# An attention and gated-convolution kernel: weights decoded two chunks per instruction, and the smaller part of x made in PSUM for two units

## Chip, cores and metric

The kernel runs on one core of a Trainium2 chip. What counts is the device time of one execution in microseconds (us), from outside; beside it stands the span, from the first to the last instruction of a profiled execution.

## Reference

Attention over a sliding window of 64 positions, then a feed-forward block with a three-tap convolution as gate. All data are float32; the weights arrive as 64-bit floats (two 32-bit words each) and are decoded on the chip.

```python
def _attn_ref(q, k, v):                      # batch 8, heads 8, seq 576, head_dim 64
    scores = scale * np.matmul(q, k.transpose(0, 1, 3, 2))
    mask = (rel >= 0) & (rel < 64)
    scores = np.where(mask, scores, -1000000000.0)
    scores = scores - np.max(scores, axis=-1, keepdims=True)
    attn = np.exp(scores)
    attn = attn / (np.sum(attn, axis=-1, keepdims=True) + 1e-09)
    return np.matmul(attn, v)
def _moe_ref(x, w_in, conv_w, w_out):        # x: (8, 576, 512), d_ff 1024
    h = np.maximum(x @ w_in, 0.0)
...
    for k in range(K):
        conv_out += conv_w[k][None, None, :] * hp[:, k:k + S, :]
    gate = 1.0 / (1.0 + np.exp(-conv_out))
    return (h * gate @ w_out)
```

## The kernel before

**Units and stages.** The 4608 rows of x are worked in 12 units of 384 rows. Of each unit, `scores` (L538) multiplies queries by keys, `row_max` (L559, VectorE) adds the mask and takes the maximum, `exps` (L569, ScalarE) makes exponentials and their sums, `guard`, `reciprocal` and `normalise` (L575 to L588) divide, and the result is turned so that keys lie on the partitions: for units 0 and 1 by TensorE (`turn`, L595) and a copy out of PSUM (`unturn`, L600), for the later ones by VectorE (`transpose`, L607) and 12 small DMAs (`place`, L620). `values` (L627) then makes x, one of four chunks c of 128 features per PSUM bank.

**Split operands.** TensorE works on float32r here, a float32 of fewer bits, so every operand is split into a larger and a smaller part. `split_hi` (L632) copies the bank of x to `xh` on ScalarE or VectorE, and `split_lo` (L637) subtracts `xh` from the bank on VectorE and writes `xl`. `mm1` (L644) is 12 matmuls for one of eight chunks f of d_ff: larger times larger, larger weight-rest times larger x, and larger weight times `xl`. Then come `relu` (L670, L672), the convolution (`conv_mid`, `conv_side`, L686 to L693), `sigmoid` (L697), `gate` (L704), the split of the gated values (`gate_hi` L709, `gate_lo` L714) and `mm2` (L723, L728), three matmuls per piece. `result` (L733) copies the banks out, and SyncE stores them.

**Decoding a weight chunk.** A chunk f of w_in or w_out is 128 by 512 numbers, each two words. `load_w` (L426) fetches it; then `magnitude` (L438 ScalarE or L440 VectorE), `shift` (L444, VectorE), `sign` (L448, VectorE), `low` (L451, ScalarE), `add_low` (L455, VectorE), `larger` (L471, any of three engines) and `lo` (L475, VectorE or GpSimd). In `DECODE` the first two chunks of w_in stand alone, all others in pairs; of a pair only `shift` is one instruction, the rest are one per chunk. The decoded chunk takes the memory of its raw words.

**Order.** `plan()` lists every piece of work, and the string `ORDER` gives the order in which they are written out, by number; a letter after a number picks the engine (A ScalarE, D VectorE, P GpSimd), `/n` the PSUM bank, and `F5/0` stands for 5 matmuls on spare data (`fill`, L404). Each engine works its own part of this list strictly in order, and SyncE's part is the order of the loads. Tasks go: unit 0 with chunks 0 to 3, unit 1 with chunks 0 to 3, unit 0 with 4 to 7, unit 1 with 4 to 7, then units 2 to 11 whole. So decoding, the attention of units 0 to 3 and the first matmuls all lie in the first 90 us.

Of the kernel before, what the change touches and what calls it, by code (L numbers as in the profile page):

```python
# [15 lines left out]
P = 128  # L16
# [6 lines left out]
NT = 6  # L23
# [14 lines left out]


# [83 lines left out]
def plan():  # L123
# [126 lines left out]
    224P 240 93P 151A 77/1 231 225 70 152P 75D 232 76 213 78D 226P 468 79 146A 316 73 199 242 215P 233P 206 82  # L250
    F5/2 94/0 147D 241 207P 249 119A 234 120D 123 243P 216 83 121 208/4 250 105/1 122 251 235D 252A 209A 217D
    469 84 128 127 153/7 168 317A 244 200 85 253 245P 96D 318A 106D 107A 254D 3 321 227/5 108 110A 218/6 319
    236/4 155A 111 219A 255/0 326 109 473/2 228A 112 470 246/1 256A 325 367 113 260/7 346 124 169 129 257/0 396
    125P 474 237A 258D 114P 247A 259 261A 475 F3/6 263/1 158A 477 262 266/0 270 320 484/2 327 126D 156/7 264A
    633 322 267A 345 115A 328D 323P 265 170A 268 116P 130A 485 269/1 174 486 157A 161A 131D 179 159 509/2 479
    329D 133/5 171A 324D 634 271A 162 272/0 366 476 172 472 487 173 178 478 290/7 175 273A 480D 163 490 274D 488
    275 136 481 635 160 277A 397 293/1 482P 510 489 471 511 176A 491A 512 278 134/6 177P 492 483 164 132/4 180
    495 137 279 639/2 372 636 165D 369A 135 520 276 166A 330/0 493D 181A 280 167D 513 182P 640 183 508 185 291
    494 281P 186 292D 368A 501 188 641 351 500 184 514 370 507 187 294A 376 502 282A 650/2 371 505 295A 283P
# [100 lines left out]
def attention_moe(ctx: ExitStack, tc: tile.TileContext, q, k, v, first, w_in, conv_w, w_out, out):  # L360
# [96 lines left out]
    def part(buf, j):  # L457
        return wx[buf][:, j * DM:(j + 1) * DM]
# [391 lines left out]
```

## Time and profile before

| | us |
|---|---|
| median of 3 runs | 514.12 (513.76 to 515.83) |
| the profiled execution | 513.32 |
| its span | 511.5 |
| TensorE (PE) busy | 499.8 |
| VectorE (DVE) busy | 398.7 |
| ScalarE (ACT) busy | 327.1 |
| GpSimd (POOL) busy | 169.2 |

The profiled execution took 513.32 us, 1.8 us more than its span and 0.8 us less than the median of the runs. In the rows below PE is the matmuls and PEld the loads of their stationary operand; times are in us from the start of the span, and L is a line of the kernel. What stands in brackets behind a row is the engine's idle time just before it and what ended it. The duration of an instruction on DVE and ACT overlaps the start of the next, so the price of one in a full queue is the distance between two starts.

### The profile page before, as it was taken

The numbers are of one execution on the slowest core, as the hardware profiler recorded it, in microseconds if no ns is written. First come the engines' busy times: TensorE is split into PE (matmuls) and PEld (weight loads), VectorE is DVE, ScalarE is ACT, GpSimd is POOL, SyncE is SP. The second block draws the span as 40 slices with busy tenths as digits, with TensorE's granted clock in tenths as the row PEclk, the third lists the DMA queues.
The fourth block names the chain that finished last, engine by engine and source line by source line (L and its number), as shares of the span: only waits on it lengthen the run. The fifth ranks groups of instructions, "written<-read, shape, count | busy, mean of one in ns | idle before, by whom it ended". The sixth has DMA issues, their size and how long they took to land.

```text
span 511.5 us, 13953 instructions
## 1 busy us (share of the span) xinstructions
PE 499.8 (98%) x5375; PEld 438.2 (86%) x5375; DVE 398.7 (78%) x1197; ACT 327.1 (64%) x923; POOL 169.2 (33%) x254
## 2 busy tenths in 40 slices
PE   8798999999999999999999999999999999999997
PEld 5587978998888898898888889988889889898996
DVE  5999999997996986597667858887386778846682
ACT  5999999967837863855864874572792675242330
POOL 6766452430441442511332532121344131152020
PEclk9999999999999999999999999999999999999999
DMA  8996635082634533804642613806263303410011
GB/s 326 405 408 216 257 84 146 6 288 85 161 104 114 175 70 105 261 4 125 212 144 70 219 62 112 258 14 197 59 254 110 108 13 113 124 62 33 0 63 62
DMA packets 27570, 71.98 MB, mean 141 GB/s; under 512 B 5744, under 2 KB 14064, under 8 KB 27504
## 3 DMA queue, kind: packets, MB, share of 16 engines
q1 hardware_dynamic: 27216, 69.52, 40.8%
q0 software_dynamic: 288, 1.57, 1.8%
q8 instruction: 42, 0.69, 0.6%
q14 instruction: 24, 0.20, 0.1%
HBM read 48.26 MB, written 11.01 MB: 116 GB/s over the span
## 4 chain that ended last, share of the span: by engine, by line
PE 87%; DVE 9%; POOL 2%; issue 1%; ACT 0%; POOLq 0%
PE bank L723 36%; PE bank L644 36%; PE bank L627 7%; PE bank L538 5%; PE bank L728 3%; DVE s L559 2%; DVE c L693 1%; DVE wx L448 1%; DVE xl L637 1%; POOL s L588 1%; DVE wx L455 1%; DVE s L588 1%; DVE wx L444 0%; ACT s L569 0%; POOL mask L493 0%
## 5 line engine op out<-in xcount | busy, mean ns | idle before, releaser
L644 PE MATMUL bank<-xh,w_in 128*128 128x384 f32 x768 | 197.5, 338 | 0.0
L723 PE MATMUL bank<-w_out,gh 128*128 128x512 f32 x528 | 168.8, 401 | 0.0
L644 PEld LDWEIGHTS bank<-xh,w_in 128*128 128x128 f32 x768 | 138.8, 188 | 7.0
L693 DVE SCALAR_TENSOR_TENSOR c<-hbuf,cw,c 128x386 f32<-128x386 f32 (+1 forms) x192 | 125.0, 674 | 13.8 <-ACT c L686 12.5
L644 PE MATMUL bank<-xl,w_in 128*128 128x384 f32 x384 | 129.0, 336 | 0.9 <-DVE xl L637 0.9
L569 ACT ACTIVATE s<-s,nm 128x96 f32<-128x96 f32 (+2 forms) x288 | 105.2, 368 | 17.1 <-DVE nm L559 16.9
L723 PEld LDWEIGHTS bank<-w_out,gh 128*128 128x128 f32 x528 | 96.0, 188 | 19.0 <-POOL w_out L475 0.2
L723 PE MATMUL bank<-w_out,gl 128*128 128x512 f32 x264 | 104.2, 395 | 0.2 <-DVE gl L714 0.2
L704 POOL TENSOR_TENSOR c<-c,hbuf 128x386 f32<-128x386 f32 (+5 forms) x39 | 44.8, 1166 | 110.4 <-ACT c L697 110.4
L559 DVE CUSTOM_DVE_ANT_0 s<-bank,mask 128x96 f32<-128x96 f32 (+2 forms) x288 | 56.6, 255 | 29.3 <-PE bank L538 25.1
L644 PEld LDWEIGHTS bank<-xl,w_in 128*128 128x128 f32 x384 | 72.1, 188 | 1.3 <-DVE xl L637 1.3
L697 ACT ACTIVATE c<-c 128x772 f32<-128x772 f32 (+1 forms) x48 | 40.6, 849 | 35.6 <-DVE c L693 35.3
L714 POOL TENSOR_TENSOR gl<-c,gh 128x768 fp32r<-128x768 f32 (+1 forms) x22 | 42.5, 1930 | 57.5 <-DVE gh L709 32.0
L723 PEld LDWEIGHTS bank<-w_out,gl 128*128 128x128 f32 x264 | 49.5, 188 | 12.2 <-DVE gl L714 0.6
L569 ACT ACTIVATION_READ_ACCUMULATOR s<-s,nm 128x1 f32 x288 | 54.6, 189 | 0.0
L670 ACT ACTIVATE hbuf<-bank 128x384 f32<-128x384 f32 x55 | 26.0, 484 | 44.1 <-PE bank L644 41.8
L588 POOL TENSOR_TENSOR s<-s,r 128x768 f32<-128x768 f32 (+1 forms) x22 | 30.1, 1376 | 62.0 <-DVE r L581 57.8
L686 ACT ACTIVATE c<-hbuf,cw 128x386 f32<-128x386 f32 (+1 forms) x57 | 34.1, 613 | 17.2 <-POOL gl L714 6.4
L627 PEld LDWEIGHTS bank<-ub,v 128*64 128x64 f32 x1152 | 35.6, 138 | 8.2 <-issue 4.4
L538 PEld LDWEIGHTS bank<-qk 64*32 64x32 f32 (+1 forms) x2112 | 29.6, 110 | 13.3 <-issue 6.6
L627 PE MATMUL bank<-ub,v 128*64 128x64 f32 x1152 | 38.7, 224 | 1.3 <-ACT ub L600 1.3
L538 PE MATMUL bank<-qk 64*32 64x96 f32 (+2 forms) x2112 | 38.2, 253 | 1.0 <-DMA qk<-in_first_dram 0.6
(78 smaller groups left out, 538.0 us busy)
## 6 DMA issues: line engine op xcount, KB each, us to landing
v<-in_v_dram SPq DMA_DIRECT2D x24, 768.0 KB, 5.5
ub<-T SPq DMA_DIRECT2D x240, 48.0 KB, 2.2
qk<-in_k_dram SPq DMA_DIRECT2D x20, 448.0 KB, 4.6
out_dram<-ot SPq DMA_DIRECT2D x11, 768.0 KB, 4.7
qk<-in_q_dram SPq DMA_DIRECT2D x20, 384.0 KB, 5.5
raw_in<-in_w_in_dram SPq DMA_DIRECT2D x8, 512.0 KB, 6.3
raw_out<-in_w_out_dram SPq DMA_DIRECT2D x8, 512.0 KB, 7.7
qk<-in_first_dram SPq DMA_DIRECT2D x12, 320.0 KB, 4.6
```

Of the source, the lines that this page charges most:

```text
L538: nc.tensor.matmul(banks[bank[h]][r:r + rows, i * P + o:i * P + k], qq[hs, s:s + rows], kk[hs, s + o:s + k], start=True, stop=True)
L559: nc.vector.tensor_tensor_reduce(out=ss[n // NB][:, n % NB, h, o:k], in0=banks[bank[h]][:, i * P + o:i * P + k], in1=mask[m][:, o:k], scal ...
L569: nc.scalar.activation(x, x, AF.Exp, bias=small(nms, (n,))[:, h:h + 1], scale=-1.0, accum_out=small(sms, (n,))[:, h:h + 1])
L588: engine[on].tensor_tensor(sv, sv, small(rs, ns).unsqueeze(2).broadcast_to([P, 2 * len(ns), k]), ALU.mult)
L627: nc.tensor.matmul(banks[bank[0]][h * D:(h + 1) * D, t * W:(t + 1) * W], vs[:, c, t, h], ub[g][:, 2 * p:2 * p + 2, 2 * t + h], start=True, ...
L644: nc.tensor.matmul(banks[bank[0]][:, :NX], w[:, a, c], y[x][:, c], start=(c == 0 and j == 0), stop=(c == NC - 1 and j == 2))
L686: nc.scalar.activation(c, h, AF.Copy, scale=w)
L693: nc.vector.scalar_tensor_tensor(c, h, w, c, op0=ALU.mult, op1=ALU.add)
L697: nc.scalar.activation(both(u, j), both(u, j), AF.Sigmoid)
L704: engine[on].tensor_tensor(c[:, :, a:a + n], c[:, :, a + o:a + o + n], h[:, :, 1 + a + o:1 + a + o + n], ALU.mult)
L714: engine[on].tensor_tensor(gls[j % 3][:, :, :n], cs[j % 2][:, :, :n], ghs[j % 3][:, :, :n].bitcast(F32), ALU.subtract)
L723: nc.tensor.matmul(banks[bank[0]], x, wts["out", f][:, w], start=(start and i == 0), stop=(stop and i == 2))
```

## The change

Of a pair of chunks, every step of the decoding becomes one instruction over both (1024 numbers per partition instead of 512); the raw words and the decoded weights of a pair share one tile. For units 1 and 2 `split_lo` is replaced: `less` multiplies `xh` by a matrix with -1 on the diagonal and adds it to the bank of x in PSUM, and `split_rest` copies what is left, which is `xl`, on ScalarE or VectorE. To allow that, `values` marks only its first and last matmuls as start and stop. `minus` makes the matrix once, on ScalarE. The string `ORDER` is replaced as a whole.

What the two strings hold, counted: matmuls on spare data 23 before and 16 after; `lo` on GpSimd 7 chunks of 16 before, 2 chunks (both of the single ones) after; `split_rest` 5 on ScalarE and 3 on VectorE; `relu` 55 on ScalarE and 41 on VectorE before, 49 and 47 after; `result` 25 and 17 before, 32 and 10 after; `normalise` 20 on VectorE and 22 on GpSimd before, 24 and 18 after. Changes of ScalarE between exponential and sigmoid: 41 before, 35 after. The loads ahead of the first load of v are the same ones in another order.

```diff
--- before.py
+++ after.py
@@ -37,6 +37,8 @@
 BY_PE = 2
 
 
+BY_DIFFERENCE = (1, 2)
+
 NXB = 3
 SPLIT = 2
 TASKS = [(0, 0, 4), (1, 0, 4), (0, 4, 8), (1, 4, 8)]
@@ -133,12 +135,8 @@
         buf = i % 2
         for f in fs:
             at("load_w", key, f)
-        for j, f in enumerate(fs):
-            at("magnitude", key, f, buf, j)
-        at("shift", key, fs, buf)
-        for j, f in enumerate(fs):
-            for fn in ("sign", "low", "add_low", "larger", "lo"):
-                at(fn, key, f, buf, j)
+        for fn in ("magnitude", "shift", "sign", "low", "add_low", "larger", "lo"):
+            at(fn, key, fs, buf)
 
     def attention(u):
         if u < FINE:
@@ -181,10 +179,15 @@
             bank = [None]
             at("values", u, c, bank=bank)
             at("split_hi", u, c, bank=bank)
-            at("split_lo", u, c, bank=bank)
+            if u in BY_DIFFERENCE:
+                at("less", u, c, bank=bank)
+                at("split_rest", u, c, bank=bank)
+            else:
+                at("split_lo", u, c, bank=bank)
 
     at("first_masks")
     at("identity")
+    at("minus")
     for m in (1, 2):
         at("later_masks", m)
     done, decoded, turns = set(), set(), {fs: i for i, fs in enumerate(DECODE)}
@@ -242,106 +245,104 @@
 
 
 ORDER = """
...
@@ -377,6 +378,7 @@
     cbits = pool.tile([P, 3 * NF, 2], U32, name="cbits")
     mask = many(3, [P, P], F32, "mask")
     ident = pool.tile([P, P], F32, name="ident")
+    negated = pool.tile([P, P], F32R, name="negated")
     qk = pool.tile([P, FIRST], F32, name="qk")
     qs = qk[:, :NC * NX].rearrange("p (c n) -> p c n", c=NC)
     ks = qk[:, NC * NX:NC * (2 * NX + W)].rearrange("p (c n) -> p c n", c=NC)
@@ -422,8 +424,11 @@
 
     @work
     def load_w(key, f):
-        raws[key, f] = pool.tile([P, DM, 2], U32, name=f"raw_{key}{f}", tag=f"{key}{f}")
-        nc.sync.dma_start(raws[key, f].rearrange("p e two -> p (e two)"), src[key][f].bitcast(U32))
+        fs = next(fs for k, fs in DECODE if k == key and f in fs)
+        if (key, fs) not in raws:
+            raws[key, fs] = pool.tile([P, len(fs) * DM, 2], U32, name=f"raw_{key}{fs[0]}", tag=f"{key}{fs[0]}")
+        a = fs.index(f) * DM
+        nc.sync.dma_start(raws[key, fs][:, a:a + DM].rearrange("p e two -> p (e two)"), src[key][f].bitcast(U32))
 
     @work
     def load_conv():
@@ -454,25 +459,28 @@
         xu = x.bitcast(U32)
         nc.vector.tensor_tensor(xu, xu, lw, ALU.add)
 
-    def part(buf, j):
-        return wx[buf][:, j * DM:(j + 1) * DM]
-
-    fn["magnitude"] = lambda key, f, buf, j, on: to_magnitude(part(buf, j), raws[key, f][..., 1], on)
-    fn["sign"] = lambda key, f, buf, j: to_sign(part(buf, j), raws[key, f][..., 1])
-    fn["low"] = lambda key, f, buf, j: to_low(raws[key, f][..., 0])
-    fn["add_low"] = lambda key, f, buf, j: to_add_low(part(buf, j), raws[key, f][..., 0])
+    def part(buf, fs):
+        return wx[buf][:, :len(fs) * DM]
+
+    fn["magnitude"] = lambda key, fs, buf, on: to_magnitude(part(buf, fs), raws[key, fs][..., 1], on)
+    fn["sign"] = lambda key, fs, buf: to_sign(part(buf, fs), raws[key, fs][..., 1])
+    fn["low"] = lambda key, fs, buf: to_low(raws[key, fs][..., 0])
+    fn["add_low"] = lambda key, fs, buf: to_add_low(part(buf, fs), raws[key, fs][..., 0])
 
     def copy(on):
         return nc.scalar.copy if on == "ACT" else engine[on].tensor_copy
 
     @work
-    def larger(key, f, buf, j, on):
-        wts[key, f] = pool.tile([P, 2, DM], F32R, name=f"w_{key}{f}", tag=f"{key}{f}")
-        copy(on)(wts[key, f][:, 0], part(buf, j))
-
-    @work
-    def lo(key, f, buf, j, on):
-        engine[on].tensor_tensor(wts[key, f][:, 1], part(buf, j), wts[key, f][:, 0].bitcast(F32), ALU.subtract)
+    def larger(key, fs, buf, on):
+        w = wts[key, fs] = pool.tile([P, 2, len(fs) * DM], F32R, name=f"w_{key}{fs[0]}", tag=f"{key}{fs[0]}")
+        for j, f in enumerate(fs):
+            wts[key, f] = w[:, :, j * DM:(j + 1) * DM]
+        copy(on)(w[:, 0], part(buf, fs))
+
+    @work
+    def lo(key, fs, buf, on):
+        w = wts[key, fs]
+        engine[on].tensor_tensor(w[:, 1], part(buf, fs), w[:, 0].bitcast(F32), ALU.subtract)
 
     @work
     def shift(key, fs, buf):
@@ -504,6 +512,10 @@
     @work
     def identity():
         make_identity(nc, ident)
+
+    @work
+    def minus():
+        nc.scalar.activation(negated, ident, AF.Copy, scale=-1.0)
 
     @work
     def later_masks(m):
@@ -625,7 +637,7 @@
         for t in range(NT):
             for h in range(2):
                 nc.tensor.matmul(banks[bank[0]][h * D:(h + 1) * D, t * W:(t + 1) * W], vs[:, c, t, h],
-                                 ub[g][:, 2 * p:2 * p + 2, 2 * t + h], start=True, stop=True)
+                                 ub[g][:, 2 * p:2 * p + 2, 2 * t + h], start=(t == 0), stop=(t == NT - 1))
 
     @work
     def split_hi(u, c, on, bank):
@@ -635,6 +647,15 @@
     def split_lo(u, c, bank):
         x = x_of(u)
         nc.vector.tensor_tensor(xl[x][:, c], banks[bank[0]][:, :NX], xh[x][:, c].bitcast(F32), ALU.subtract)
+
+    @work
+    def less(u, c, bank):
+        nc.tensor.matmul(banks[bank[0]][:, :NX], negated, xh[x_of(u)][:, c], start=False, stop=True,
+                         skip_group_check=True)
+
+    @work
+    def split_rest(u, c, on, bank):
+        copy(on)(xl[x_of(u)][:, c], banks[bank[0]][:, :NX])
 
     @work
     def mm1(u, f, bank):
```

## Rows read from the trace of the kernel before

**Rows 1.** The page: busy time by engine, and the granted TensorE clock in 40 equal slices, in tenths.
```profile
PE 499.8 (98%) x5375; PEld 438.2 (86%) x5375; DVE 398.7 (78%) x1197; ACT 327.1 (64%) x923; POOL 169.2 (33%) x254
PEclk9999999999999999999999999999999999999999
```

**Rows 2.** Stretches of the span: length, then the busy time of each engine with its instructions, the granted clock, the share of DMA time, GB/s.
```profile
5.50:22.40 16.90, 12.82 (x201) 8.53 (x193) 16.57 (x103) 15.60 (x69) 11.47 (x27) 1.00 1.03 402
22.40:47.40 25.00, 22.61 (x405) 19.94 (x402) 24.79 (x81) 24.15 (x72) 16.28 (x29) 1.00 0.83 320
47.40:65.00 17.60, 17.52 (x210) 15.50 (x208) 17.53 (x59) 16.65 (x52) 8.22 (x8) 1.00 0.69 260
65.00:490.00 425.00, 424.92 (x4437) 373.72 (x4438) 329.11 (x943) 265.55 (x726) 125.51 (x170) 1.00 0.38 117
490.00:511.50 21.50, 17.93 (x101) 17.47 (x99) 10.19 (x15) 3.83 (x6) 3.58 (x2) 1.00 0.19 73
```

**Rows 3.** The chain of work that ended last, in order of time: start, length, what.
```profile
5.48 0.29 DVE s L559
...
63.29 0.87 DVE s L588
64.15 0.88 DVE gl L714
65.03 0.04 issue
65.08 3.97 PE bank L723 x16
...
75.08 0.93 PE bank L538 x56
...
86.31 1.55 PE bank L627 x48
...
488.18 2.10 PE bank L644 x12
...
491.50 16.44 PE bank L728 x93
```

**Rows 4.** TensorE's instructions in order of time: start, length, what, and in brackets the idle time before it.
```profile
22.40 1.62 PE L627 MATMUL bank<-ub,v 128*64 128x64 f32 x48
23.95 0.51 PE L404 MATMUL bank<-spare 128*128 128x512 f32 x1
24.39 1.62 PE L627 MATMUL bank<-ub,v 128*64 128x64 f32 x48
26.02 1.43 PE L404 MATMUL bank<-spare 128*128 128x512 f32 x5
27.28 0.51 PE L644 MATMUL bank<-xh,w_in 128*128 128x384 f32 x2
...
29.27 0.44 PE L644 MATMUL bank<-xl,w_in 128*128 128x384 f32 x1 [0.94 <-DVE xl L637]
...
40.48 0.96 PE L404 MATMUL bank<-spare 128*128 128x512 f32 x3
42.73 1.62 PE L627 MATMUL bank<-ub,v 128*64 128x64 f32 x48 [1.29 <-ACT ub L600]
```

**Rows 5.** Everything that TensorE waited for from 42.73 to 508 us: total, times, longest.
```profile
PE bank L627 <- ACT ub L600: 1.3, 1, 1.3
PE bank L723 <- DVE gl L714: 0.2, 1, 0.2
```

**Rows 6.** VectorE's instructions in order of time (start, length, what), three pieces of the queue.
```profile
43.98 0.68 DVE L448 SCALAR_TENSOR_TENSOR wx<-raw_in,wx 128x512 uint32<-128x512 uint32 x1
44.57 0.68 DVE L455 CUSTOM_DVE_ANT_0 wx<-raw_in,wx 128x1024 uint16<-128x1024 uint16 x1
45.18 0.68 DVE L475 TENSOR_TENSOR w_out<-wx,w_out 128x512 fp32r<-128x512 f32 x1
45.78 0.68 DVE L455 CUSTOM_DVE_ANT_0 wx<-raw_in,wx 128x1024 uint16<-128x1024 uint16 x1
46.38 0.42 DVE L471 CAST w_in<-wx 128x512 fp32r<-128x512 f32 x1
46.72 1.01 DVE L637 TENSOR_TENSOR xl<-bank,xh 128x384 fp32r<-128x384 f32 x2
47.65 0.24 DVE L559 CUSTOM_DVE_ANT_0 s<-bank,mask 128x96 f32<-128x96 f32 x1
...
55.07 0.42 DVE L688 TENSOR_SCALAR c<-hbuf,cw 128x386 f32<-128x386 f32 x1
55.52 0.62 DVE L693 SCALAR_TENSOR_TENSOR c<-hbuf,cw,c 128x386 f32<-128x386 f32 x1
...
63.20 0.95 DVE L588 TENSOR_TENSOR s<-s,r 128x768 f32<-128x768 f32 x1
64.07 0.95 DVE L714 TENSOR_TENSOR gl<-c,gh 128x768 fp32r<-128x768 f32 x1
```

**Rows 7.** ScalarE's instructions in order of time (start, length, what), two pieces of the queue.
```profile
30.85 0.67 ACT L451 ACTIVATE raw_out<-raw_out 128x512 uint32<-128x512 uint32 x1
31.41 0.39 ACT L569 ACTIVATE s<-s,nm 128x128 f32<-128x128 f32 x1
...
39.58 1.28 ACT L697 ACT_TABLE_LOAD   x1
40.87 0.85 ACT L697 ACTIVATE c<-c 128x772 f32<-128x772 f32 x1
```

**Rows 8.** Groups by line and shape over the whole span: count, busy time, mean ns of one, idle time before.
```profile
L644 PE MATMUL bank<-xh,w_in 128*128 128x384 f32 x768 | 197.5, 338 | 0.0
L672 DVE TENSOR_SCALAR hbuf<-bank 128x384 f32<-128x384 f32 x41 | 22.3, 547 | 10.8 <-PE bank L644 10.7
```

More of the change, by code (lines that the diff above doesn't have):

```diff
@@ L250 @@
[L250 to L259, printed above, removed]
@@ L340 @@
[L340 to L344 removed]
+    3 7 98 81 5 6 9 87 143 10 0 F5/0 32/2 8 96 82 14 133 33 4 99A 134 102 100 35 101 F3/0 13/4 83 103 23/6 104D
@@ new lines @@
+    474 601 277/1 444 366 260A 445D 261A 309A 278 446 451 127/4 161 280/7 476 310D 264A 602 155A 435 163 450
+    129/6 281A 130 262 453 265 132 343A 454D 156D 311/0 477 455 263 603 164A 456D 606/2 266 475 457 314/7 313A
+    344 267 470 165D 462 459 345 166 466 346 168 467 268P 608 279A 465 169 282A 471 463 171 315A 607 172A 469
+    167 347 269A 468 617/2 174A 270D 478 170 764 348P 618 460 273/6 619 464 271/4 173A 479D 461 480 481D 274
+    285A 316A 276 482 611 272/5 349D 489 622 641/2 487 612 283 350/0 765 328A 286 493 287 485 623 284 492 329
@@ new lines @@
+    1059A 1076 1308 1077 1261 1171/0 1060P 1316 1318 1288 1437/2 1284 1172A 1078 1285 1189/7 1439 1287 1079P
+    1438 1310 1314 1461/2 1293 1080A 1313 1063 1170A 1081P 1462 1441 927 1066 1463 1315 1062 1289 1191D 1426/2
+    1291 1173A 1286 1176A 1061 1442 1312 1177 1064 1178 1440 1311 1192/0 1194D 1584 1443 1195 1174 1294 1444P
+    1309 1082 1193A 1295 1197A 1210/1 1464 1319 1198 1175 1292 1466 1199 1260 1467 1065 1445 1317 1428 1446P
+    1179 1083 1585 1085 1213/7 1180D 1196 1333 1084 1200 1181D 1087 1232 1427 1212A 1182P 1432 1086 1214D 1586
@@ new lines @@
+    1771 1620 1525D 1394 1769 1522D 1614 1523 1541/1 1770 1619 1790 1772A 1540D 1543A 1410 1542D 1526 1411 1524
+    1413 1527 1754/2 1773 1416D 1528 1414 1544 1912 1545 1412 1755 1793 1648/7 1529P 1756 1657/0 1649D 1650
+    1654/1 1774P 1792 1415 1655D 1913 1758 1656 1511/4 1760 1530D 1559/7 1531P 1658A 1418A 1759 1546A 1661
+    1562/1 1561D 1417A 1682 1547 1757 1419 1914 1795 1761D 1762 1753 1651/7 1796A 1564A 1563D 1659 1567A 1514
+    1652D 1653 1513/6 1763D 1512/5 1797 1764 1516 1798P 1660/1 1548 1775 1549 1915 1788 1515 1786 1662D 1663/0
@@ new lines @@
+    1823 1846 1933 1579 1957 1919 1675/4 1819A 1582D 1936A 1959 1578 1816D 1707D 1958 1723/1 1708 1694A 1711
+    1817 1956 1581D 1677/6 1922 1960P 1820 1726/7 1709 1920 1961 1712 1923 1695D 1680 1924 1676/5 1937 1921
+    1725D 1727D 1812/0 1925P 1731A 1678 1713 1813D 1938D 1698 1814 1701 1962D 1728A 1696 1732 1679 1729 1697
+    1952 1700 1733 1963 1699 1824/1 1926 1714D 1975 1730 1715A 1867 1927D 1827/7 1716P 1928 1939 1845/0 1826D
+    1941 1828A 1734 1940 1832A 1973 1735D 1916 1717 1847A 1833 1583 1736A 1719 1950 1829A 1848/1 1945 1737D 1946
@@ new lines @@
+    1830 1971 1834 1942 1831 1720 1850D 1967 1835 1738 1949 1849A 1718 1836P 1721 1866/7 1853D 1837A 1851 1966
+    1838P 1974 1722 1868D 1964 1869/0 1972 1854 1852 1965 1917 1740 1947 1870D 1871D 1741 1948 1872 1970 1739
+    1855 1744A 1943 1743 1874D 1951 1742 1746A 1944 1856 1839/4 1745D 1969 1887/1 1875 1968 1857D 1876 1842
+    1858D 1873 1840/5 1859P 1877 1841/6 1843 1890/7 1878P 2012 1860 1989 1888 1844 1889A 1891A 1976/0 1982/1
+    1985/7 1983D 1892D 1862 1986A 1977D 1879D 1861 1984 1863 1880D 1979/1 1978 1893 1864 1980A 1895A 1882 1896
@@ new lines @@
+    1885 1897 1865 1981 1894 1881 1987 1898 1884 1988/0 1899P 2035 2058 1991/1 1990A 1900A 1901P 2011/7 1992D
+    1996D 1902 2013D 1993D 1883 2016A 1994 1903 1997 2014/0 1995 1998 1999 2000P 1905 2015D 2034/1 1908A 2001A
+    2002D 1886 2036A 1904 2039A 1906 2040 1907 2019D 2017 2006/7 2041 2037/0 2020 2021 2018 2057/1 2038A 2022
+    2042A 2023D 2003/4 2043 2024A 2060/0 2044 2025P 1909D 2010 2061A 2004/5 1910A 2065D 2008 2045 2059D 1911
+    2029 1747 2062A 2046D 2007 2033 2063 2026 2064 2030 2047D 2005/6 2066 2009 2048D 2027 2031 2067 2028 2068
@@ L345 @@
+    2052 2069D 2049 2053 2070D 2056 2071D 2050 2054 2032 2051 2073 2075 2077 2055 2079 2074 2088 2086 2082D 2078
+    2087 2089 2072 2084D 2083 2076 2085 2080A 2081
 """
```

155 lines of the change are left out of this document (65 added, 90 removed).

## Prediction

> **What bounds the kernel now.** I read the page first: TensorE is busy for 98% of the span, at the full granted clock in every slice [rows 1]. Such a share says little by itself, so the stretches come next. From 65 to 490 us TensorE is busy for 424.92 of 425.00 us, while VectorE is busy for 329.11 and ScalarE for 265.55 [rows 2]. There only TensorE's own work counts, and a cheaper instruction on another engine is worth nothing. From 5.5 to 65 us it is the other way round: VectorE is busy for 16.57 of 16.90, 24.79 of 25.00 and 17.53 of 17.60 us [rows 2], and the chain lies mostly on VectorE up to the `gate_lo` at 64.15, after which it stays on TensorE [rows 3]. The list of TensorE's waits agrees: after 42.73 us it waits for 0.2 us more, and then never until 508 [rows 5]. So the time is a start, in which VectorE sets when TensorE may go on, plus TensorE's work, plus the last store. What TensorE loses in the start after its first `values` can be read off: three groups of spare matmuls, 23.95 to 24.39, 26.02 to 27.28 and 40.48 to about 41.44 (0.44 + 1.26 + 0.96), and waits of 0.94 and 1.29 [rows 4] and 0.2 [rows 5]: 5.1 us. That is all a better start can give after 22.4 us; the clock has nothing to give.
>
> **The merged steps.** `sign`, `add_low` and `lo` of 512 numbers start 0.60 us apart (43.98, 44.57, 45.18, 45.78, 46.38), and two-input work on 768 numbers takes 0.87 (63.20 to 64.07) [rows 6]. The slope is 0.27 us for 256 numbers, which leaves 0.06 us that does not depend on size, so 1024 numbers should take 1.14 us instead of 1.20. The bounds are a saving of nothing and of 0.6 us a pair (the second half free); I take 0.06, since both rows show time growing with size. `larger` takes 0.34 us (46.38 to 46.72), and I give `magnitude` on VectorE the same; a pair of either is put at 0.6. On ScalarE, `low` takes 0.56 us (30.85 to 31.41) [rows 7]; a pair can save between nothing and 0.56, and this costs or gains nothing as long as VectorE is the later of the two.
>
> The Trainium skill, Perfetto Trace Analysis, "Optimizing Scalar/DVE Operations", puts the access overhead of a DVE instruction on SBUF at about 60 ns, which the 0.06 us above agrees with; the same section says that where an engine is not saturated but makes another one wait, breaking instructions up may let work finish sooner, which speaks against merging. By the first sentence nine merges ahead of unit 1's first matmul give some 0.5 us, by the second the price is that of the rival on pairs below.
>
> **VectorE's queue up to unit 1's first `mm1`.** I count both `ORDER` strings by kind. Before, VectorE's last needed work is the `split_lo` that ends by 47.65 [rows 6]; its queue since 5.48 [rows 3] holds 40.8 us by these distances, the rest of the 42.2 us being idle time and small gaps. Unchanged are row maxima, copies of turned blocks, reciprocals and `split_hi`. What differs up to the same step:
> `sign` and `add_low`, 16 single (9.60) become 4 single and 6 double (2.40 + 6.84): -0.36;
> `lo`, 2 single become 2 double, since those of chunk 0 and 1 stay on GpSimd: +1.08;
> `magnitude`, 4 single become 1 single and 1 double: -0.4;
> `split_lo`, 8 at 0.465 (46.72 to 47.65 for two [rows 6]) become 4 plus one `split_rest` of 0.47: -1.4;
> two `relu` move to ScalarE, 0.46 each (0.547 on average [rows 8], less the 0.08 by which starts lie closer): -0.9;
> one `normalise` moves to GpSimd: -0.6;
> two `conv_mid` at 0.45 (55.07 to 55.52) and one `conv_side` at 0.53 are pulled ahead [rows 6]: +1.4.
> The sum is -1.2: 39.6 instead of 40.8. TensorE's work ahead of this step is 34.8 us before (`scores` 0.93 and `values` 0.775 by the chain [rows 3], `mm1` 2.10, and the same turns), and 35.5 after, with four `less` in it. So VectorE's lead, which TensorE has to wait out, falls from 6.0 to 4.1 us here. Counted the same way through the whole start, the largest lead before is this 6.0, and after it is 4.3, at unit 1's second `gate_lo` (75.9 us of VectorE's work against 71.6 of TensorE's). The step is worth **-1.7 us**, with bounds of nothing (idle time in the new queue takes it back; before it was 0.5 us from 5.5 to 47.4 [rows 2]) and of the whole 5.1.
>
> ScalarE's part of the same start gets shorter too: before, TensorE's 1.29 us wait is for an `unturn` [rows 4] that stands behind a table load of 1.28 and a sigmoid of 0.85 [rows 7]; in the new string the first sigmoid follows unit 1's copies. That is no extra gain, since VectorE's lead covers the same microseconds. `minus` is one ScalarE instruction long before `less`; ScalarE's idle time covers it, 1.3 of 16.9 us there [rows 2], and without that cover it costs some 0.3. The loads ahead of v keep their bytes, at 402 GB/s [rows 2], so v lands no later; first chunks of w_in move ahead of unit 1's queries and those come later by about 1 MB, 2.5 us, under row maxima of unit 0.
>
> **The eight `less`.** Each is one more matmul of 128x384. In `mm1` 12 take 2.10 us [rows 3], 0.175 each: **+1.4 us**. If none overlaps its neighbour, it is the 0.338 of the row [rows 8], 2.7 us. I take 1.4, as each stands between other matmuls. This is work on the engine that bounds everything after the start, so nothing hides it.
>
> **From 80 us on.** Neither the number nor the shapes of TensorE's other matmuls change. `relu` moves to VectorE, `result` to ScalarE, and `gate_lo` keeps its shares; VectorE has 96 us to spare from 65 to 490 [rows 2]. I take 0, with a bound of +3 for new waits. The end keeps its shape (16.44 us of `mm2` [rows 3], a copy, a store): 0.
>
> **Sum.** -1.7 + 1.4 = -0.3 us. The profiled execution would go from 513.32 to 513.0; its 513.32 lies 0.8 below the median of the runs, so the median goes from 514.1 to **513.8 us**. A change under 0.5% (2.6 us) can hardly be told from none here.
>
> **Rivals.**
> (a) *The start closes up entirely.* All 5.1 us of spare matmuls and waits after 22.4 us go, only `less` is paid: -5.1 + 1.4, 510.4 us. For it: the waits on ScalarE and on VectorE both have less work ahead of them, and 7 spare matmuls are gone. Against it: VectorE still has 4 us of lead, and it is as full as before. 0.25.
> (b) *TensorE waits at `less`.* It is strictly in order, and `less` of a chunk needs that chunk's `split_hi`, a copy in the full queues of VectorE or ScalarE. Before, nothing on TensorE stood between `values` and `mm1` that needed the copy. Behind a waiting `less` stand scores, `mm1` and `mm2` of other units. Between `values` and `less` the new string puts 0.8 us (unit 1, chunk 3) to 2.1 us of other matmuls; the copy takes 0.47, so it decides from the point where it starts more than 0.3 us after `values` ends, that is behind a single `conv_side` of 0.53. If all eight come 0.6 late: +4.8 - 0.3, 518.6 us. For it: VectorE's idle share of 1% [rows 2]. Against it: lateness that is already in VectorE's lead is not paid twice. 0.11.
> (c) *A pair is late as a whole.* The first chunk is ready only with the second: `sign`, `add_low`, `larger` and `lo` end after 1.14 x 3 + 0.6 = 4.0 us instead of 2.1. Where this decides twice, for instance at w_out 2 and 3 and w_in 6 and 7, it costs 3.8 - 0.3: 517.6 us. For it: TensorE needs the first chunk of a pair first. Against it: `lo` of w_in 2 and 3 stands some 3 us of VectorE's work ahead of its `mm1`. 0.07.
>
> The forecast has 0.57. Faster by over 0.5% is (a), 0.25; within 0.5% is the forecast, 0.57; slower is (b) and (c), 0.18. The likeliest case alone lies between 511.6 and 516.5. For 8 in 10 the range takes in (a) and (c): 510.4 to 517.6.
>
> **What would show it.** VectorE's last `split_rest` or `split_lo` of unit 1 should end 0.5 to 2 us earlier than 47.65; single starts of merged `sign` and `add_low` should lie 1.14 us apart; the eight `less` should take some 0.18 us each with no wait before them; and spare matmuls and waits after the first `values` should sum to about 3.4 us instead of 5.1. The forecast is wrong if waits at `less` or at `mm2` show, if TensorE waits after 100 us, or if with fewer spare matmuls the granted clock falls to its lower level, 1.2 GHz, in the start, where TensorE idles longest.

## The result and the profile after

The changed kernel takes 518.75 us (median of 5 runs, 517.98 to 520.31) against 514.12 before: 1.0092 times as long, with an interval of 1.0065 to 1.0118. By the ratio it is slower by 4.7 us (3.3 to 6.1), where 0.3 us less was forecast, and it lies above the range. Its profiled execution has a span of 517.0 us (before 511.5).

The page, busy time by engine and the granted clock in 40 slices, answering [rows 1]:
```profile
PE 501.1 (97%) x5376; PEld 439.8 (85%) x5376; DVE 396.5 (77%) x1179; ACT 319.5 (62%) x897; POOL 161.8 (31%) x251
PEclk9889999999999999999999999999999999999999
```
TensorE is busy for 1.3 us more and idle for 15.9 us instead of 11.7: 4.2 of the 5.5 us are idle time. The busy time holds more than it shows: seven spare matmuls fewer (0.25 us each by the 1.26 us for five in [rows 4]) and eight `less` more (0.175 each by the forecast) would make it 0.35 us shorter, so by this estimate some 1.6 us of it are work that took longer. The clock row has two slices under 9 where it had none.

Stretches, as in [rows 2]: length, busy time of TensorE, weight loads, VectorE, ScalarE and GpSimd with their instructions, granted clock, DMA share, GB/s:
```profile
5.50:22.40 16.90, 10.76 (x144) 7.42 (x143) 14.43 (x83) 14.36 (x63) 14.22 (x33) 0.90 0.99 387
22.40:47.40 25.00, 22.13 (x392) 19.86 (x392) 23.24 (x88) 22.25 (x78) 11.74 (x14) 0.93 0.85 319
47.40:65.00 17.60, 17.60 (x212) 16.04 (x211) 17.46 (x56) 16.99 (x42) 5.63 (x11) 1.00 0.76 283
65.00:490.00 425.00, 423.81 (x4486) 371.39 (x4485) 326.80 (x935) 258.00 (x705) 124.12 (x169) 1.00 0.38 115
17.00:22.00 5.00, 5.00 (x50) 4.00 (x51) 4.43 (x18) 4.86 (x21) 4.31 (x6) 0.66 0.98 390
```
In the first two rows together VectorE is busy for 37.67 instead of 41.36 us. Both stretches have a fixed length, so this says only that it stands idle for 3.7 us more; it does not say that it has less to do. What it has to do shows when one counts to the same step, the end of the last split of unit 1's x, before (first row) and after:
```profile
5.48:47.65 42.17, 35.70 (x604) 28.74 (x597) 41.63 (x184) 40.00 (x140) 28.01 (x56) 1.00 0.91 353
5.33:50.13 44.80, 35.80 (x606) 29.77 (x604) 40.57 (x172) 39.48 (x147) 26.10 (x49) 0.92 0.90 344
```
VectorE's work up to there fell by 1.1 us, much as forecast (1.2), but its idle time rose from 0.5 to 4.2 us, and the step ends 2.5 us later. GpSimd, which had 11.47 us of work up to 22.4, has 14.22. The stretch from 17 to 22 us shows TensorE at a granted clock of 0.66: part of the 5 us at its lower level, 1.2 GHz. From 30 to 33 and from 33 to 36 us it is 0.80 and 0.64.

The largest of TensorE's waits over the whole span: total, times, longest; the last row is the kernel before:
```profile
PE bank L607 <- POOL s L600: 6.1, 4, 3.7
PE bank L550 <- DMA qk<-in_first_dram: 2.3, 4, 1.1
PE bank L665 <- DVE hbuf L693: 0.7, 1, 0.7
...
PE bank L595 <- POOL s L588: 3.1, 4, 1.2
```
The largest is for GpSimd (`normalise`, L600; the `turn` that waits is L607), an engine that the forecast's sum did not contain. It has grown by 3.0 us. GpSimd's queue in order of time:
```profile
5.60 0.20 POOL L497 MEMSET mask<- 128x128 f32 x1
5.88 0.26 POOL L501 TENSOR_SCALAR_AFFINE_SELECT mask<-mask 32x96 f32<-32x96 f32 x1
...
10.23 0.12 POOL L506 MEMSET mask<- 32x32 f32 x1
10.44 1.27 POOL L483 TENSOR_TENSOR w_in<-wx,w_in 128x512 fp32r<-128x512 f32 x1
11.79 0.23 POOL L589 TENSOR_SCALAR sm<-sm 128x4 f32<-128x4 f32 x1
12.33 1.13 POOL L600 TENSOR_TENSOR s<-s,r 128x512 f32<-128x512 f32 x1 [0.30 <-DVE r L593]
13.40 0.48 POOL masks.py:197 MEMSET ident<- 128x128 f32 x1
...
15.57 1.36 POOL L600 TENSOR_TENSOR s<-s,r 128x512 f32<-128x512 f32 x1
```
The third mask (`later_masks(2)`, which units 0 and 1 do not read) is built from 5.60 to 10.35, in front of GpSimd's first `guard` and `normalise`, which unit 0's turns need. How long it takes stood in the trace of before, 5.7 us, where the same mask is built thirty microseconds later:
```profile
35.69 0.21 POOL L489 MEMSET mask<- 128x128 f32 x1
...
41.30 0.12 POOL L498 MEMSET mask<- 32x32 f32 x1
```
VectorE at the same time, and at a second place, at 25 us:
```profile
12.06 0.18 DVE L593 RECIPROCAL r<-sm 128x4 f32<-128x4 f32 x1 [1.80 <-POOL sm L589]
...
24.52 0.73 DVE L449 TENSOR_SCALAR wx<-wx 128x1024 uint32<-128x1024 uint32 x1
25.29 1.23 DVE L453 SCALAR_TENSOR_TENSOR wx<-raw_in,wx 128x1024 uint32<-128x1024 uint32 x1
26.55 1.23 DVE L460 CUSTOM_DVE_ANT_0 wx<-raw_in,wx 128x2048 uint16<-128x2048 uint16 x1
...
27.76 0.37 DVE L593 RECIPROCAL r<-sm 128x4 f32<-128x4 f32 x3
```
Here three steps of the pair 2,3 of w_in, 3.2 us together, stand ahead of three reciprocals of unit 1. And TensorE:
```profile
16.98 1.09 PE L607 MATMUL bank<-ident,s 128*128 128x128 f32 x8 [3.69 <-POOL s L600]
...
24.82 1.62 PE L639 MATMUL bank<-ub,v 128*64 128x64 f32 x48
...
30.02 0.63 PE L607 MATMUL bank<-ident,s 128*128 128x128 f32 x4 [1.55 <-POOL s L600]
...
33.19 0.99 PE L665 MATMUL bank<-xh,w_in 128*128 128x384 f32 x2
```
The first `values` begin at 24.82 (before 22.40, [rows 4]), the first `mm1` at 33.19 (before 27.28); three turns of unit 1 stand ahead of it in the new order and none in the old.

### The profile page after: what moved, and what is told of

Its sections match the earlier page's. It is cut to its first block, busy times and chain, and to the rows that moved or that the text cites. A ratio compares the mean times of both kernels' runs of the same rounds, so it can differ in the third digit from the quotient of the medians.

```text
span 517.0 us, 13894 instructions
## 1 busy us (share of the span) xinstructions
PE 501.1 (97%) x5376; PEld 439.8 (85%) x5376; DVE 396.5 (77%) x1179; ACT 319.5 (62%) x897; POOL 161.8 (31%) x251
## 4 chain that ended last, share of the span: by engine, by line
PE 85%; DVE 6%; ACT 4%; POOL 3%; issue 1%; POOLq 0%; DVEq 0%
PE bank L665 35%; PE bank L744 34%; PE bank L639 6%; PE bank L550 5%; PE bank L749 3%; DVE c L714 1%; ACT s L581 1%; DVE s L571 1%; POOL s L600 1%; PE bank L607 1%; DVE wx L453 1%; DVE wx L460 1%; DVE wx L449 0%; ACT hbuf L691 0%; ACT c L718 0%
## 5 line engine op out<-in xcount | busy, mean ns | idle before, releaser
L714 DVE SCALAR_TENSOR_TENSOR c<-hbuf,cw,c 128x386 f32<-128x386 f32 (+1 forms) x192 | 123.4, 668 | 18.2 <-ACT c L707 17.0
L581 ACT ACTIVATE s<-s,nm 128x96 f32<-128x96 f32 (+1 forms) x288 | 105.2, 369 | 5.7 <-DVE nm L571 5.4
L725 POOL TENSOR_TENSOR c<-c,hbuf 128x386 f32<-128x386 f32 (+5 forms) x43 | 48.0, 1133 | 143.2 <-ACT c L718 143.2
L691 ACT ACTIVATE hbuf<-bank 128x384 f32<-128x384 f32 x49 | 23.6, 488 | 59.1 <-PE bank L665 53.8
L693 DVE TENSOR_SCALAR hbuf<-bank 128x384 f32<-128x384 f32 x47 | 25.7, 550 | 22.5 <-PE bank L665 22.4
```

The costliest lines, as they stand in the source:

```text
L581: nc.scalar.activation(x, x, AF.Exp, bias=small(nms, (n,))[:, h:h + 1], scale=-1.0, accum_out=small(sms, (n,))[:, h:h + 1])
L693: engine[on].tensor_scalar_max(out, ps, 0.0)
L714: nc.vector.scalar_tensor_tensor(c, h, w, c, op0=ALU.mult, op1=ALU.add)
L725: engine[on].tensor_tensor(c[:, :, a:a + n], c[:, :, a + o:a + o + n], h[:, :, 1 + a + o:1 + a + o + n], ALU.mult)
```

## The experiments

All ratios are to the kernel before, run beside each kernel on the same chip; the kernels ran on several chips, so they are compared with one another through their ratios. Behind a difference of two ratios stands a range, from the two intervals by the root of the sum of squares. One thing limits what single traces say: the fourth group of scores began at 7.99 us in the trace of before and at 9.44 in that of another kernel with the same load queue (last section), and 1.2 us of this difference are left in the two spans. So a shift of some 1 us between two traces says little, and verdicts go by the ratios.

**GpSimd's queue, the clock, and `less`, in the changed kernel.** Four kernels. The first moves the third mask:
```diff
 GpSimd: ... first_masks, carry(0,0), blank(0)
-        later_masks(2)
         lo(in 1), guard, normalise, identity, ..., carry(0,3)
+        later_masks(2)
```


> The changed kernel with one piece of work moved in GpSimd's queue: the third mask, needed only by unit 3, is made after the third carry instead of ahead of the first guard. Theory G (the new order of GpSimd's queue delays the first guard and normalise, VectorE and TensorE wait, TensorE's clock then falls): the mask takes 4.75 us from 5.60 to 10.35 in the changed kernel, the guard at 11.79 comes some 2 us earlier, VectorE's 1.80 us of idle time goes, TensorE's 3.69 us wait shrinks to under 2, and the end comes 2 to 4.5 us earlier than the 518.8 of the changed kernel: 514.3 to 516.8. Theory L (the eight extra matmuls and waits for the copies ahead of them): no change, 518 to 519.5. Theory M (pairs of weight chunks come late as a whole): no change.

1.0034 (1.0018 to 1.0050), 516.76 us. In its trace the first two rows below are those of the 16.98 and the 30.02 above:
```profile
15.29 1.51 PE L602 MATMUL bank<-ident,s 128*128 128x128 f32 x8 [1.88 <-POOL s L595]
...
28.31 0.63 PE L602 MATMUL bank<-ident,s 128*128 128x128 f32 x4 [1.40 <-POOL s L595]
...
31.46 0.99 PE L660 MATMUL bank<-xh,w_in 128*128 128x384 f32 x2
```
The mask's place cost some 3.0 us by the ratios (1.4 to 4.6). It is the largest cause found by moving one piece of work; whether it is larger than the price of the clock, below, the ranges do not say. The wait of 3.69 us does not vanish; 1.88 us stay.

The second goes further along the same queue:
```diff
 GpSimd: as masks_later, and
-        lo(in 1), ..., identity behind the first normalise
+        identity ahead of all guards, lo(in 1) behind the fifth normalise
```


> As the run with the mask moved, and two more moves in GpSimd's queue: the identity matrix is made right after the first blank, in idle time, and the lo of w_in chunk 1 (1.27 us) after unit 0's fifth normalise. Theory G: the first normalise starts at about 8.5 us instead of 12.33, TensorE's first turn at about 13 instead of 16.98, the granted clock stays at 1.00 from 17 to 36, and the time is 512.5 to 515. Theories L and M: 518 to 519.5, as the changed kernel.

1.0055 (1.0038 to 1.0071). In this kernel `lo` of chunk 1 of w_in reads its buffer after the next pair's magnitudes were written there, so that this chunk's smaller part is another number; the instructions are the same. At 517.29 us this misses the 512.5 to 515 expected. The first turn stays at 15.32 us, because the first `normalise` now waits for VectorE's reciprocal:
```profile
10.48 1.12 POOL L595 TENSOR_TENSOR s<-s,r 128x512 f32<-128x512 f32 x1 [1.74 <-DVE r L588]
```
So behind the mask VectorE's queue is the limit at this place, and emptying GpSimd's further gives nothing.

The third adds spare products where TensorE stood idle:
```diff
-F4 ahead of the first turn;                                F1
+F20 ahead of the first turn; F6 ahead of unit 1's turns;   F4
```


> The changed kernel with spare matmuls put into TensorE's waits: 20 instead of 4 ahead of the first turn, 6 ahead of unit 1's first turn, 4 instead of 1 ahead of its third. Order and waits of all other work are as in the changed kernel. If the lower clock costs time by itself (granted 0.66 from 17 to 22, 0.80 from 30 to 33, 0.64 from 33 to 36 us), 1 to 3.4 us come back: 515.4 to 517.8. If the waits for GpSimd alone set the time, nothing changes: 518 to 519.5.

1.0050 (1.0034 to 1.0065), 517.12 us, with the mask where the changed kernel has it. Its stretches:
```profile
5.50:22.40 16.90, 14.81 (x179) 10.76 (x181) 15.56 (x85) 14.16 (x62) 13.65 (x34) 0.90 1.00 386
17.00:22.00 5.00, 5.00 (x62) 3.90 (x64) 4.45 (x20) 4.77 (x20) 3.83 (x6) 1.00 1.01 389
```
The granted clock stays at 1.00 from 17 us on. The 0.90 of the first row comes from 8 to 13 us, behind a wait of 1.81 us for a load in this execution, where spare products and scores run at the lower level. Products of zeros alone gave back 2.2 us by the ratios (0.6 to 3.8). They do no work of the kernel and nothing waits for their result, so this is what TensorE had lost after its idle time by running at the lower level. The changed kernel's own executions go the same way: 517.98 us at a mean granted clock of 0.996, 520.08 and 520.31 at 0.989 and 0.990.

The fourth takes `less` out again:
```diff
-BY_DIFFERENCE = (1, 2)      less, split_rest
+BY_DIFFERENCE = ()          split_lo at the place of split_rest
```


> The changed kernel with the old split_lo on VectorE in the place of less and split_rest for units 1 and 2, order otherwise the same. Theory L in its strong form (TensorE waits at less): 3 us or more come back, under 516. Only the work of eight matmuls of 0.175: 517.3. Theory G: between 517.3 and 519.5, since five subtractions of 0.47 us come back to VectorE, which is full in the start.

1.0111 (1.0092 to 1.0129), 520.32 us: slower than the changed kernel by 1.0 us by the ratios, with a range on both sides of zero (-0.7 to 2.6). In this order `less` is not the loss; whether it pays is not shown.

**Each edit alone in the old order.** The next question was whether the edits or the new order cost the time. One kernel has the merged decoding, with the engines that it has in the changed kernel, one has `less` alone, both in the order of before:
```diff
 the kernel before, its ORDER
-magnitude, sign, low, add_low, larger, lo: one instruction a chunk
+the same for a pair, each at the place of the later chunk's step
+(pair 6,7 of w_in and 2,3 of w_out near the first one's place)
-lo of five chunks (w_in 3 and 6, w_out 2, 3 and 7) on GpSimd
+the same within a pair, on VectorE
```


> The kernel before with the pairs decoded by one instruction a step and nothing else: its own order, each merged step where the later of its two single steps stood (for the pair 6,7 of w_in and 2,3 of w_out, which are wanted soon, low, add_low, larger and lo near the first one's place), engines as in the changed kernel. Theory O (merging costs nothing by itself; the new order of the queues lost the time): 513.5 to 515, and the third mask, still where it was before, keeps the first turns where they were (11.48, 13.67, 15.49 us). Theory M (merging costs by itself: nothing of a pair is there until both chunks are through, and a 1.2 us instruction stands in front of a reciprocal): 515.5 to 518, with mm1 of chunk 2 or of unit 1 waiting for `lo` of a pair.

1.0054 (1.0036 to 1.0073): +2.8 us. Theory O falls. Some waits of TensorE in its trace that the kernel before does not have:
```profile
53.40 0.50 PE L717 MATMUL bank<-w_out,gh 128*128 128x512 f32 x1 [0.41 <-DVE w_out L469]
...
68.67 0.50 PE L717 MATMUL bank<-w_out,gl 128*128 128x512 f32 x1 [0.61 <-DVE gl L708]
...
115.67 0.50 PE L717 MATMUL bank<-w_out,gh 128*128 128x512 f32 x1 [0.76 <-DVE w_out L469]
```
Two of the three are for `lo` of a pair of w_out: the first chunk is there only with the second, rival (c) of the forecast, and it decides as late as 115 us. (Decoding goes on to about 110 us in the kernel before too, not only to 90.) These two are 1.2 us. Where the rest of the 2.8 us comes from is open. The kernel does not merge alone: `lo` of five chunks, which GpSimd had done, is now VectorE's, and at 0.60 us each [rows 6] that is 3.0 us more for the engine that sets the pace. No run takes this apart from the merging.

```diff
 the kernel before, its ORDER
-split_lo(u, c) for u = 1, 2
+less(u, c), split_rest(u, c) at the same place; minus once
```


> The kernel before with x's smaller part of units 1 and 2 made by `less` on TensorE and a copy from PSUM, in place of the subtraction on VectorE, in its own order, and nothing else; the copies run on ScalarE for chunks 0, 1 and 3 (unit 1) and 0 and 3 (unit 2), as in the changed kernel. If `less` pays as it did inside the changed kernel (1.6 us over split_lo there): 512.5 to 513.8, with VectorE's last step of unit 1's x earlier. If TensorE pays for eight more products and gets nothing back (the sum of the forecast's `less` term): 515.3 to 516. Between, 514 to 515: the cover of VectorE's lead hides both.

1.0080 (1.0060 to 1.0100): +4.1 us, more than any case expected. TensorE and VectorE:
```profile
43.85 0.45 PE L648 MATMUL bank<-xh,negated 128*128 128x384 f32 x1 [1.75 <-DVE xh L639]
```
```profile
50.84 0.56 DVE L653 CAST xl<-bank 128x384 fp32r<-128x384 f32 x1 [2.73 <-PE bank L648]
```
TensorE waits at `less` for `split_hi` (rival (b)), and VectorE stands still before a `split_rest`, because the `less` that it needs is queued behind a whole `mm1`. The next run moved these steps:
```diff
 less_old_order, unit 1
-less(1,0), split_rest(1,0), fill, values(1,2)
+fill, values(1,2), less(1,0), split_rest(1,0)
-split_rest(1,2) on VectorE, row_max (4,5), row_max (6,7)
+row_max (4,5), row_max (6,7), split_rest(1,2)
```


> less_old_order with two changes of order in unit 1: the first `less` (chunk 0) and the copy after it behind the next chunk's products with v, and the copy of chunk 2's smaller part on VectorE behind two row maxima of unit 2 instead of ahead of them. In less_old_order TensorE waited 1.75 us at the first `less`, and VectorE stood 2.73 us before that copy. Theory W (the price of `less` is the waits that it puts into two strict queues, not its own 8 products of 0.175 us): 1.2 to 2.7 us below less_old_order's ratio of 1.008, at 1.003 to 1.0055 of the kernel before. Rival (the price is its products and later copies): within 0.5 us of less_old_order.

1.0111 (1.0085 to 1.0137): nothing gained, rather more lost. Its trace starts like that of before (first `mm1` with a smaller part at 29.28 and 29.27), so the two can be laid side by side. TensorE in this kernel:
```profile
47.83 0.62 PE L660 MATMUL bank<-xh,w_in 128*128 128x384 f32 x2 [1.17 <-ACT xl L653]
...
51.01 0.61 PE L660 MATMUL bank<-xh,w_in 128*128 128x384 f32 x2 [0.47 <-DVE xl L653]
...
82.23 0.92 PE L634 MATMUL bank<-ub,v 128*64 128x64 f32 x24
...
132.12 1.62 PE L634 MATMUL bank<-ub,v 128*64 128x64 f32 x48
```
and in the kernel before the answering `values`:
```profile
78.94 0.92 PE L627 MATMUL bank<-ub,v 128*64 128x64 f32 x24
...
126.63 1.62 PE L627 MATMUL bank<-ub,v 128*64 128x64 f32 x48
```
The waits went elsewhere: 1.17 us at an `mm1` that writes the very PSUM bank in which a chunk of x still stood until ScalarE had copied its rest, and ScalarE had a table load of 1.28 us and two exponentials in front of that copy. The lag is 0.2 us at 42.95, 3.3 at 82 and 5.5 at 132; from there on it is constant (5.4 at the end). The chain `values`, `split_hi`, `less`, `split_rest`, `mm1` has one step more than `values`, `split_hi`, `split_lo`, `mm1`, goes back to TensorE for it, and holds its bank until the copy; here, moving two of its steps inside strict queues moved the waits.

What eight products cost without that chain:
```diff
 the kernel before, values(u, c) for u = 1, 2
+one product of zeros, 384 columns, into the chunk's bank, ahead of the first
```


> The kernel before with eight products more and nothing else: ahead of each chunk's products with v in units 1 and 2, one product of zeros over the same 384 columns that `less` has, into the same PSUM bank, which nobody reads before it is overwritten; no `less`, no new copy. It measures what eight more products cost TensorE without any new chain. Own price (the forecast's term, 8 x 0.175): +1.4 us, ratio 1.0027; then of the 4.1 us that less_old_order lost, 2.7 are the new chain's waits. If they are hidden in TensorE's waits of the start (1.29 us at unit 1's products with v): 0.3 to 1.0 us.

1.0037 (1.0022 to 1.0052): +1.9 us (1.1 to 2.7), in agreement with 8 x 0.175 = 1.4. So of the 4.1 us some 2 are the products, and the other 2.2 (0.9 to 3.5) are left for the chain and its copies, by subtraction.

```diff
 the kernel before, its ORDER
+pairs_old_order and less_old_order together
```


> The kernel before with both edits, pairs_old_order and less_old_order together, each step at its old place: the change without its new order. If the prices add (2.8 and 4.1 us): ratio 1.011 to 1.0145, that is 1 to 2.5 us slower than the changed kernel, and the new order then gave back part of what the edits cost. If the edits free one another (VectorE's subtraction gone makes room for the pairs): 1.006 to 1.009, and the new order itself gave nothing.

1.0145 (1.0125 to 1.0165): +7.5 us, about the sum of 2.8 and 4.1. The edits do not make room for one another in the old order; the new order, with the mask in the wrong place, still gave back some 2.7 us of it (1.0 to 4.4).

**Mending the new order.** Three kernels, one on the other:
```diff
 masks_later
 VectorE:  +guard and reciprocal of unit 1's burst (4,5) ahead of sign of pair 2,3 (w_in),
           +reciprocals of (0,1) and (2,3) between its sign and its add_low
 ScalarE:  +guards of (0,1) and (2,3) as early
 GpSimd:   +three normalises of unit 1 ahead of larger of that pair
```


> The changed kernel with the third mask behind the third carry (as in masks_later, 516.8) and, on VectorE, the guards and reciprocals of unit 1's bursts (0,1), (2,3) and (4,5) ahead of sign and add_low of the chunk pair 2,3; on GpSimd the three normalises of these bursts ahead of `larger` of that pair. Theory Q (the pair's steps, 1.23 us each, stand as blocks in strict queues in front of what unit 1's turns wait for): unit 1's first turn comes about 2.5 us earlier than the 28.31 us of masks_later, the waits of 1.40 and 0.33 us before the turns go, mm1 of unit 0 begins near 29.5 instead of 31.46, and the time is 1 to 2 us below masks_later (514.8 to 515.8). Rival T (the turns stand in front of mm1 in TensorE's queue, but what mm1 and the later work wait for is something else: VectorE's whole load up to there): first mm1 earlier, but the gain is given back by 45 us, 516.3 to 517.3.

1.0034 (1.0018 to 1.0049): the same as masks_later. GpSimd and VectorE at that place:
```profile
25.42 4.85 POOL L595 TENSOR_TENSOR s<-s,r 128x512 f32<-128x512 f32 x3 [0.98 <-DVE r L588]
```
```profile
25.20 1.19 DVE L448 SCALAR_TENSOR_TENSOR wx<-raw_in,wx 128x1024 uint32<-128x1024 uint32 x1
26.31 0.23 DVE L588 RECIPROCAL r<-sm 128x4 f32<-128x4 f32 x2
26.46 1.91 DVE L455 CUSTOM_DVE_ANT_0 wx<-raw_in,wx 128x2048 uint16<-128x2048 uint16 x1
```
The normalises do begin earlier, and then take 1.6 us each where two of them take 2.04 in the changed kernel at 28.89, with `larger` ahead of them; the pair's add_low beside them takes 1.91 instead of 1.23. TensorE still waits 1.88 us at unit 1's first turn (30.29 in this trace), where theory Q had no wait left. So theory Q falls: moving these reciprocals ahead of the long steps gave back no time.

```diff
 recip_first
-F4, -, F1
+F12 ahead of the first turn, F5 ahead of unit 1's first turn, F2
```


> recip_first, and the spare products of the first gap 12 instead of 4, five more before unit 1's first turn, two instead of one in the third place: TensorE idles less and its granted clock stays at 1.0 from 17 us on. Theory C (beside the queues, what is left over the kernel before is the lower granted clock after TensorE's long idle times; the spare products gave 1.6 us when put alone into the changed kernel): 0.5 to 1.5 us below recip_first, 513.7 to 515. Rival (the clock's price was the same time as the queues' waits, counted twice): within 0.4 us of recip_first.

1.0025 (1.0009 to 1.0041). The clock is 1.00 from 17 us on, and the step over recip_first, 0.5 us (-0.7 to 1.6), is not larger than its uncertainty. TensorE waits again later:
```profile
67.42 0.50 PE L739 MATMUL bank<-w_out,gh 128*128 128x512 f32 x1 [0.88 <-DVE w_out L478]
78.06 0.45 PE L660 MATMUL bank<-xh,w_in 128*128 128x384 f32 x1 [0.19 <-DVE w_in L478]
84.58 0.62 PE L660 MATMUL bank<-xh,w_in 128*128 128x384 f32 x2 [0.70 <-DVE hbuf L688]
```
```diff
 all_fixes, VectorE
+lo of w_out 2,3 and lo of w_in 6,7 each ahead of a transpose of unit 2;
+relu of chunks 6 and 7 of unit 0 ahead of sign, and of a row maximum
```


> all_fixes, with four steps moved forward in VectorE's queue: `lo` of pair 2,3 of w_out ahead of a transpose of unit 2, `lo` of pair 6,7 of w_in ahead of the next transpose, relu of chunk 6 of unit 0 ahead of `sign` of pair 4,5 of w_out, relu of chunk 7 ahead of a row maximum. In all_fixes TensorE waited for just these: 0.88 us at 67.42, 0.19 at 78.06, 0.70 at 84.58. Theory S (what the start gives back is lost again between 60 and 100 us to the order of VectorE's steps, not to the sum of its work): these three waits are gone, 1.3 to 1.8 us below all_fixes. Rival V (VectorE, 99% busy from 60 to 100 us, sets the pace by its sum): other waits of the same sum take their place, within 0.5 us of all_fixes.

1.0048 (1.0029 to 1.0066). The three waits are gone and others came:
```profile
70.92 1.16 PE L545 MATMUL bank<-qk 64*32 64x96 f32 x64 [1.15 <-DVE nm L566]
...
91.44 0.92 PE L634 MATMUL bank<-ub,v 128*64 128x64 f32 x24 [1.97 <-DMA ub<-T]
```
Theory S falls. That VectorE sets the pace by its sum (rival V) fits: it is busy for 19.86 of the 20 us from 60 to 80 in both kernels, and what is pulled ahead pushes something else back (here a row maximum, and unit 2's transposes with the transfers behind them that place its blocks). But the time is 1.2 us above all_fixes (-0.1 to 2.4), where V said within 0.5, so V is argued and not shown.

```diff
 lo_relu_first (all_masks), and the kernel before (before_masks); GpSimd
-later_masks(1), ..., first_masks
+first_masks, later_masks(1)
```


> lo_relu_first, and on GpSimd the mask that unit 0 reads made first, ahead of the one of the later units: the first row maximum, which in every kernel so far waits for this mask till 5.3 to 5.5 us, can begin by 4.5. If VectorE's first steps set the start, 0.4 to 0.9 us below lo_relu_first; if the loads of queries and keys do (TensorE waits 1 to 2 us for them in this stretch), within 0.3.

> The kernel before with only the order of its first two masks on GpSimd exchanged, the one of unit 0 first. As with all_masks: 0.4 to 0.9 us under the kernel before if VectorE's first row maximum sets the start, 0.2 or less if the loads do. This is the candidate to be faster than both kernels.

1.0061 (1.0038 to 1.0083) and 1.0006 (0.9990 to 1.0023): nothing. No version tried is faster than the kernel before.

## Why the prediction was wrong

**The step that failed: "-1.7 us" for VectorE's lead.** The count of work behind it was right: up to the end of the last split of unit 1's x VectorE's work fell by 1.1 us, with 1.2 forecast. But its worst case was a gain of nothing ("idle time in the new queue takes it back; before it was 0.5 us"), and the same idle time is 4.2 us after, 3.7 more, so the step became a loss. A count of work in a strict queue gives the end of that queue only if nothing in it waits, and I counted one engine's queue and took the others' as given. I also took the stretch ahead of 22.4 us as given ("all a better start can give after 22.4 us"), and the first `values` begin 2.4 us later than that. VectorE's last `split_rest` of unit 1 begins at 49.66 and ends by 50.13, not 0.5 to 2 us ahead of 47.65.

**Where it failed first: GpSimd's queue.** It was counted by name (one `normalise` more) and not in order. The third mask ahead of the first `guard` was in the new `ORDER`, and its 5.7 us in the trace of before. It cost about 3 us (masks_later, 1.4 to 4.6), with a share of the clock in it.

**The clock: named, not priced.** "If with fewer spare matmuls the granted clock falls" stood among the signs; it fell (0.66 from 17 to 22 us) and is worth some 2 us (more_spare, 0.6 to 3.8). This overlaps the mask's 3 us and is not added to it.

**The merges: the term was mis-sized by its kind.** The durations were nearly right: sign and add_low of a pair follow each other at 1.26 and 1.14 us (1.14 forecast). But the price is not the duration: with the changed kernel's engines they cost 2.8 us in the old order. Some 1.2 us of it are waits by rival (c), to which I gave 0.07; the rest is open between the long blocks and the five `lo` that moved to VectorE. That the blocks cost by standing ahead of short, urgent steps is not shown: recip_first moved such steps ahead of them and gained nothing, though its normalises also took longer. The second sentence that I cited from the Trainium skill (Perfetto Trace Analysis, "Optimizing Scalar/DVE Operations") pointed the right way, but its condition, an engine that is not saturated, did not hold: VectorE was busy for 24.79 of 25.00 us there [rows 2].

**`less`: products right, chain missing.** +1.4 us for eight products agrees with products_only (+1.9, 1.1 to 2.7). In the changed kernel no `less` has a wait before it, so rival (b) did not happen there, although its 518.6 lies close to the result. In the old order it did happen (1.75 us). The new chain is left with about 2 us there, while in the new order taking `less` out gained nothing (no_less, 1.0 us slower, -0.7 to 2.6): its worth hangs on what the queues look like, and the forecast gave it one price.

**Nothing from 80 us on: wrong by about 1 us.** TensorE was idle for 1.2 us between 65 and 490 us (0.08 before), 0.9 of it after 80, in waits for VectorE's `lo` of w_in and `relu`. From 150 to 490 us it was never idle, and the end was as forecast.

**Loads "come later by about 1 MB, under row maxima": no cost shown.** TensorE waits 2.3 us for queries and keys of unit 0 (0.6 before), and in the new string one chunk of w_in does stand ahead of five of unit 0's six first loads, before ahead of three. But over all traces this wait is 0.6 to 2.4 us in the seven kernels with the old order of loads and 0.5 to 2.8 in the nine with the new one, so the difference lies within the scatter of the first loads.

**How it adds up.** By the ratios: both edits in the old order +7.5, the new order -2.7, total 4.7; and of these some 3 are the mask's place. With mask, reciprocals and spare products mended 1.3 us (0.5 to 2.1) remain. That is about the price of the eight products, but no run shows that it is theirs. Whether an order exists in which the two edits gain stays open: 1.0025 was the best tried.

## What to carry to other kernels

A saving on the engine that sets the pace is worth something only if the queue stays full; so count the idle time of the new queue as well as its work, and read every other strict queue in order, above all for long work that nobody needs yet. Before merging two instructions, ask who needed the first half, and which engine does the work afterwards. A step sent back through another engine to relieve a full one costs a place in that engine's queue and holds its buffer longer, so its price depends on the order it lands in as well as on its duration.

## What the runs showed of the hardware

GpSimd and VectorE held each other up. Multiplying 128x512 took GpSimd 1.02 us where VectorE ran row maxima, a copy and subtractions from a PSUM bank (two in 2.04 at 28.89 in the changed kernel), 1.36 at 15.57 beside the add_low of one chunk, and 1.6 in recip_first beside a pair's sign and add_low; the add_low itself went from 1.23 to 1.91, while the sign took 1.19. The Trainium skill, SBUF — State Buffer, "Who interferes with whom", says that a VectorE instruction with two SBUF inputs contends with a GpSimd instruction that reads SBUF, and calls the port pair that they share an exclusive lock; recip_first agrees. By that rule one merged instruction would shut GpSimd out for about twice as long at a stretch, which no run here measured by itself.

After 3.69 us without work TensorE's granted clock in the changed kernel was 0.66 from 17 to 22 us. It did not fall at once: it was 1.00 from 17 to 18 us, 0.50 from 19 to 21 and 1.00 again from 22 on, and eight turns took 1.09 us at 16.98 and 1.97 at 19.01. The time at which the first loads land differed by at least 1.4 us between executions with the same load queue; the fourth group of scores in before_masks and, second, in the kernel before:
```profile
9.44 0.57 PE L533 MATMUL bank<-qk 64*64 64x64 f32 x16 [1.85 <-DMA qk<-in_first_dram]
...
7.99 0.56 PE L538 MATMUL bank<-qk 64*64 64x64 f32 x16
```
